# Attention: the ninth transposed block goes to spare columns of the last score bank, and VectorE's row, logit and gating work stands between its two passes

## The chip, the cores and the metric

The kernel runs on one core of one Trainium2 chip. The metric is device time in microseconds for one execution of the whole program, as the median of several runs. The engines are named as the profile names them: PE (TensorE matmul), PEld (its weight loads), DVE (VectorE), ACT (ScalarE), POOL (GpSimd), SP (the engine that issues most DMAs).

## What is computed

Three layers follow one another. The first is an attention with a threshold: 4 batches, 8 heads, 576 tokens, head size 64.

```python
scores = scale * np.matmul(q, k.transpose(0, 1, 3, 2))
thresh = np.max(scores, axis=-1, keepdims=True) - tau
scores = np.where(scores >= thresh, scores, -1000000000.0)
attn = np.exp(scores - np.max(scores, axis=-1, keepdims=True))
attn = attn / (np.sum(attn, axis=-1, keepdims=True) + 1e-09)
x = np.matmul(attn, v)            # then 2304 rows of 512
```

The second layer sends each of the 2304 rows to two of eight experts (logits of the row, noise, the best two), and the third is a dense layer with a hidden size of 2048. The change touches the attention and the choice of experts, not the matmuls of the layers behind them.

## The kernel before

The attention (the loop over `i` at L738) runs over 80 **units**. A unit is one batch, one chunk of 128 query rows and one pair of heads; 64 units have two heads (`nh` is 2), and 16 "t" units take 64 left-over rows of both heads of a pair as one tile of 128 rows (`nh` is 1). The first 16 units belong to batch 0 and have a shorter evacuation of their own (L470). Four units of one chunk make a **tile** `T` of 128 rows; there are 18 tiles.

A unit goes through these steps, each at the line named:

- `s_mm` (L350, matmuls at L364): scores of 576 columns per head, 288 in each of two PSUM banks of a `ps_s` tile. The tag has two such tiles; a two-headed unit takes both.
- `d1` (L369, DVE at L375): one pass per head reads `ps_s`, writes the scaled scores to memory and gives the row maximum. It is the only reader of `ps_s`, so it frees it for the next unit's `s_mm`.
- `a1` (L382, ACT at L386): exponentials. `thresh` (ACT, L380): the row's threshold.
- `d2` (L394, DVE at L399): the second pass, which masks by the threshold and sums the row.
- `t_mm` and `a2` (L407 and L422): the masked rows are turned by PE in blocks of 128 columns. A two-headed unit has nine blocks: parts 0 and 1 hold four each (L416), and **part 2 is the ninth block** (L418; L420 in a t unit). Each part takes a `ps_t` tile, of which the tag has three, and ACT copies it to memory (L428; L430 or L432 for the ninth block).
- `pv` (L436, PE at L449 to L454): the product with V. `group_evac` (L463) copies the finished tile out.

The steps of several units overlap, by a fixed order written out in the loop. Iteration `i` issues: `t_mm` part 0 and `a2` of unit `i - 2`, `d1` and `a1` of unit `i`, `d2` of unit `i - 1`, parts 1 and 2 of unit `i - 2`, `thresh` of `i`, `s_mm` of `i + 1`, and `pv` of `i - 3`. Every engine runs its own instructions in that order. Work beside it hangs in a table `at`, keyed by iteration and place: place 0 stands behind `s_mm`, place 1 at the end of the iteration.

For a finished tile `x_stages` (L482) puts four steps into that table, one iteration apart: `rows` (PE turns the tile at L498, DVE scales it by the inverse sums at L488, L489 and L500, SP stores it), `logits` (PE L508, ACT copy L511), `flip` (PE L515) and `sum_` (DVE L519 and L522). PE's part of each takes a `ps_t` tile too. For a group of three tiles `gating` (L532) adds the choice of experts: `top2` (DVE, L570 to L577), `rank` (PE, a `ps_t` tile) and `place` (DVE L593 and L595), then the indirect DMAs that scatter the rows (POOL L618).

After the last unit PE runs the expert and dense layers without a break to the end.

Of the kernel before, what the change touches and what calls it, by code (L numbers as in the profile page):

```python
# [14 lines left out]
HP = H // 2  # L15
# [4 lines left out]
NT = N // 128  # L20
# [5 lines left out]
DT = 2  # L26
# [7 lines left out]
def emit(tc, qt, kt, v, tau, wg, wn, noise, w1, w2, w_in, w_out, alpha, out):  # L34
# [3 lines left out]
    pe, dve, act, pool, sp = nc.tensor, nc.vector, nc.scalar, nc.gpsimd, nc.sync  # L38
# [4 lines left out]
    with (  # L43
# [56 lines left out]
        def psum_s():  # L100
            return pp.tile([128, 2, 512], FT, name="ps_s", tag="s", bufs=2)

        def psum_t(dt=FT):
            return pp.tile([128, 512], dt, name="ps_t", tag="t", bufs=3)
# [5 lines left out]
        ident = cp.tile([128, 128], FT, name="ident")  # L110
# [44 lines left out]
        rows = [c0([DM]) for _ in range(2)] + [cut(m_rows, DM * i, [DM]) for i in range(2)]  # L155
# [191 lines left out]
        NU = len(units)  # L347
        st = [dict() for _ in units]

        def s_mm(i):  # L350
            b, c, hp = units[i]
            qh, ql, kh, kl, zh, zl = sets[b * HP + hp]
            u = st[i]
            for h in range(nh(i)):
                u["ps", h] = psum_s()
            q0 = 0 if c == "t" else c * 128 + (64 if b % 2 else 0)
            for x in range(2):
                for k, (q, z, kk) in enumerate(((qh, zh, kh), (qh, zh, kl), (ql, zl, kh))):
                    for h in range(nh(i)):

                        r = slice(0, 128) if c == "t" else slice(h * 64, h * 64 + 64)
                        lhs = z if c == "t" else q[r, q0:q0 + 128]
                        o = (64 - 64 * h) + x * 288
                        pe.matmul(u["ps", h][:, x, :288], lhs, kk[r, o:o + 288], start=(k == 0), stop=(k == 2))  # L364

        def nh(i):
            return 1 if units[i][1] == "t" else 2

        def d1(i, h):  # L369
            u = st[i]  # L370
# [11 lines left out]
        def a1(i, h):  # L382
            u = st[i]
            if h == 0:
                u["em"] = em_ring()
            act.activation(u["em"][:, h], u["sp"][:, h], AF.Exp, bias=u["sm"][:, h:h + 1], scale=-1.0)  # L386
# [20 lines left out]
        def t_mm(i, part):  # L407
            u = st[i]
            em = u["em"]
            emf = em.rearrange("p h s -> p (h s)")  # L410
            ps = psum_t()
            u["pt", part] = ps
            if part < 2:
                o = part * 640
                for j in range(4):
                    pe.transpose(ps[:, j * 128:j * 128 + 128], emf[:, o + j * 128:o + j * 128 + 128], ident)  # L416
            elif nh(i) == 2:
                pe.transpose(ps[:, :128], emf[:, 512:640], ident)  # L418
            else:
                pe.transpose(ps[:64, :128], emf[:, 512:576], ident)  # L420

        def a2(i, part):  # L422
            u = st[i]
            if part == 0:
                u["P"] = pt_ring()
            ps = u.pop(("pt", part))
            if part < 2:
                act.copy(u["P"][:, 4 * part:4 * part + 4].rearrange("p a b -> p (a b)"), ps)  # L428
            elif nh(i) == 2:
                act.copy(u["P"][:, 8], ps[:, :128])  # L430
            else:
                act.copy(u["P"][:64, 8], ps[:64, :128])  # L432
# [49 lines left out]
        def x_stages(T):  # L482
            g = {}

            def inverse():
                g["inverse"] = True
                e = esum[T]
                dve.tensor_scalar(e, e, 1e-9, None, op0=OP.add)  # L488
                dve.reciprocal(e, e)  # L489

            def rows():
                x = xts[T]
                e = esum[T]
                if "inverse" not in g:
                    inverse()
                ps = psum_t()
                for c in range(HP):
                    pe.transpose(ps[:, c * 128:c * 128 + 128], x[:, c], ident)  # L498
                xtok[T] = xtok_ring()
                dve.tensor_tensor(xtok[T].rearrange("p (h d) -> p h d", h=H), ps.rearrange("p (h d) -> p h d", h=H),  # L500
                                  e[:, :, None].to_broadcast([128, H, D]), op=OP.mult)
                sp.dma_start(xd[T * 128:T * 128 + 128], xtok[T])

            def logits():
                x = xts[T]
                ps = psum_t()
                for c in range(HP):
                    pe.matmul(ps[c * 32:c * 32 + 32, :128], wcat[:, c], x[:, c], start=True, stop=True,  # L508
                              skip_group_check=True)
                g["lt"] = lt_ring()  # L510
                act.copy(g["lt"], ps[:, :128])  # L511

            def flip():
                g["ps"] = psum_t()
                pe.transpose(g["ps"][:, :128], g["lt"], ident)  # L515

            def sum_():
                t = lt_ring()
                dve.tensor_tensor(t.rearrange("p (h j) -> p h j", h=H),  # L519
                                  g["ps"][:, :128].rearrange("p (h j) -> p h j", h=H),  # L520
                                  esum[T][:, :, None].to_broadcast([128, H, 16]), op=OP.mult)
                dve.tensor_reduce(lg[:, T], t.rearrange("p (h j) -> p j h", h=H), axis=AX.X, op=OP.add)  # L522

            return [(0, 1, rows), (1, 1, logits), (2, 1, flip), (3, 0, sum_), (0, 0, inverse)]

        def bc8(ap, n):
# [5 lines left out]
        def gating(t0, t1):  # L532
# [3 lines left out]
            g = {}  # L536
# [85 lines left out]
            sends = [(T, k) for T in range(t0, t1) for k in range(2)]  # L622
            first = [exp_, one_plus, log_, noisy, top2]
            if 3 < t1 <= 12:
                plan = [(d, 1, f) for d, f in enumerate(first)] + [(5, 1, rank), (6, 0, place)]
                if t1 == FIRST:
                    plan.append((9, 0, close))
                return plan + [(6 + q, 1, lambda a=a: send(*a)) for q, a in enumerate(sends)]
            if t1 <= 15:
                plan = [(d // 2, 1, f) for d, f in enumerate(first)] + [(4, 1, rank), (5, 0, place)]  # L630
                return plan + [(5 + q // 2, 1, lambda a=a: send(*a)) for q, a in enumerate(sends)]
            if t1 == NT:

# [100 lines left out]
                f(*a)  # L734

        END = NU + DT + 1
        s_mm(0)
        for i in range(END):  # L738
            it, iv = i - DT, i - DT - 1
            tiles, outs = 0 <= it < NU, 0 <= iv < NU  # L740
            if tiles:
                t_mm(it, 0)
                a2(it, 0)
            if i < NU:
                for h in range(nh(i)):
                    d1(i, h)
                for h in range(nh(i)):
                    a1(i, h)
            if 0 < i <= NU:
                for h in range(nh(i - 1)):  # L750
                    d2(i - 1, h)
            if tiles and nh(it) == 2:
                t_mm(it, 1)
                a2(it, 1)
            if tiles:
                t_mm(it, 2)
                a2(it, 2)
            if i < NU:
                thresh(i)
            if i + 1 < NU:  # L760
                s_mm(i + 1)
            for f, a in at.pop((i, 0), []):
                f(*a)
            if i == END - 1:
                do_fill()
            if outs:
                pv(iv)
                if units[iv][2] == HP - 1 or iv < SOLO:
                    T = group_evac(iv)
                    if T is not None:  # L770
                        todo = [(i + (1, 3, 5, 7, 2)[T] + d if T < 5 else i + 1 + d, p, f) for d, p, f in x_stages(T)]
                        if T == NT - 1:
                            last_rows.append(todo[0][2])
                            todo = [(i + 1, 0, todo[1][2]), (i + 1, 0, todo[4][2]), (i + 2, 0, todo[2][2]), (i + 2, 0, todo[3][2])]
                        else:
                            todo = todo[:4]
                        if T == NT - 2:
                            todo = [(i + d, p, f[2]) for (d, p), f in zip(((1, 1), (1, 1), (2, 1), (2, 1)), todo)]
                        for t0, t1 in GROUPS:
                            if T == t1 - 1:  # L780
                                todo += [(i + {3: 8, NT - 1: 3, NT: 2}.get(t1, 4) + d, p, f) for d, p, f in gating(t0, t1)]
                        for j, p, f in todo:
                            put((j, p), f)
            if i >= NU:
                do_fill()
            for f, a in at.pop((i, 1), []):
                f(*a)
# [386 lines left out]
```

## Time and profile before

| | |
|---|---|
| median of 3 runs | 1167.44 us (1166.29 to 1167.62) |
| the profiled execution, its own time | 1170.81 us |
| its span, first to last instruction | 1169.1 us |
| PE busy | 1135.2 us (97%) |
| DVE, ACT, POOL busy | 622.8, 532.0, 532.8 us (53%, 46%, 46%) |
| granted TensorE clock, mean | 0.997 |

How it is read: the shares of busy time are averages over the attention (to about 310 us) and the layers behind it. The view by stretches gives the busy time of each engine in a stretch and the granted clock; the view of waits says who waited for whom; the timeline lists single instructions, with the idle time of the engine before them in brackets and what ended it. In a timeline a run of the same instruction is one line with its count, so the time that a step takes on PE is the distance from its start to the start of the next step.

### The profile page before, as it was taken

What the parts mean: (1) busy time and instruction counts of PE and PEld (TensorE: products, weight loads), DVE (VectorE), ACT (ScalarE), POOL (GpSimd) and SP (SyncE); (2) the same over time, 40 slices, a digit from 0 to 9 for tenths busy, and PEclk for the clock granted to TensorE, in tenths of its full rate; (3) what the DMA queues carried; (4) which work ended last, traced back from release to release, by engine and by line L of the source; (5) the groups of instructions that cost most, each with busy time, mean ns of one, the idle gap of its engine ahead of it and who ended that gap; (6) DMA issues with size and microseconds to landing.
All of it is one profiled execution on the core that took longest, in us unless ns stands there. A gap on an engine that the chain in (4) does not pass through costs nothing. (4 is left out here: it accounts for less than half of the span.)

```text
span 1169.1 us, 20453 instructions
## 1 busy us (share of the span) xinstructions
PE 1135.2 (97%) x7754; PEld 977.5 (84%) x7754; DVE 622.8 (53%) x1332; ACT 532.0 (46%) x1039; POOL 532.8 (46%) x632
## 2 busy tenths in 40 slices
PE   7999989999899999999999999999999999999997
PEld 6887777877789999999989898998888888888886
DVE  7978788899644544454545453445443343342221
ACT  7977768788624544444444454433211211211111
POOL 7636534654524545455454555556332333332221
PEclk9999999999999999999999999999999999999999
DMA  7423222132357676567667565541321321320001
GB/s 219 137 86 122 92 77 74 73 119 92 136 141 207 184 199 194 183 171 213 192 189 202 186 188 190 166 151 54 86 66 25 92 66 27 90 64 10 36 1 39
DMA packets 156552, 141.50 MB, mean 121 GB/s; under 512 B 108576, under 2 KB 109216, under 8 KB 156448
## 3 DMA queue, kind: packets, MB, share of 16 engines
q1 hardware_dynamic: 150400, 120.91, 35.1%
q0 software_dynamic: 5760, 18.88, 4.8%
q8 instruction: 63, 1.03, 0.4%
q14 instruction: 41, 0.34, 0.1%
q10 hardware_dynamic: 288, 0.34, 0.1%
HBM read 97.11 MB, written 42.99 MB: 120 GB/s over the span
## 5 line engine op out<-in xcount | busy, mean ns | idle before, releaser
L214 PE MATMUL ps_t<-m_v,m_pair 128*128 128x384 f32 (+2 forms) x1216 | 220.0, 317 | 0.3 <-DVE m_v L207 0.3
L177 POOL TENSOR_TENSOR m_pair<-m_v,m_pair 128x512 fp32r<-128x512 f32 x114 | 151.9, 1353 | 130.0 <-ACT m_pair L171 106.7
L214 PEld LDWEIGHTS ps_t<-m_v,m_pair 128*128 128x128 f32 x1216 | 186.8, 190 | 8.1 <-DVE m_v L207 0.5
L232 PE MATMUL ps_s<-m_pair,m_hh 128*128 128x512 f32 x528 | 167.5, 390 | 0.0
L995 DVE TENSOR_SCALAR m_tmp<-ps_t,alpha_t 128x512 f32<-128x512 f32 (+1 forms) x80 | 55.7, 697 | 208.6 <-PE ps_t L214 200.9
L225 DVE SCALAR_TENSOR_TENSOR m_gate<-ps_t,m_hh 128x384 fp32r<-128x384 f32 (+1 forms) x120 | 58.8, 493 | 169.9 <-ACT m_hh L224 169.8
L399 DVE SCALAR_TENSOR_TENSOR m_hh<-m_tmp,sm,m_hh 128x576 f32<-128x576 f32 x144 | 126.1, 908 | 2.4 <-ACT sm L380 2.0
L214 PE MATMUL ps_t<-m_v,m_early 128*128 128x256 f32 (+2 forms) x672 | 127.3, 320 | 0.0
L232 PEld LDWEIGHTS ps_s<-m_pair,m_hh 128*128 128x128 f32 x528 | 99.1, 188 | 20.3
L1000 POOL TENSOR_TENSOR m_v<-m_tmp,m_v 128x512 fp32r<-128x512 f32 x39 | 50.4, 1293 | 139.7 <-ACT m_v L999 139.7
L375 DVE TENSOR_SCALAR_CACHE_REDUCE m_tmp<-ps_s 128x576 f32<-128x576 f32 x144 | 103.6, 752 | 18.5 <-PE ps_s L364 16.0
L386 ACT ACTIVATE m_hh<-m_tmp,sm 128x576 f32<-128x576 f32 x144 | 105.7, 783 | 11.0 <-DVE m_tmp L375 10.9
L214 PEld LDWEIGHTS ps_t<-m_v,m_early 128*128 128x128 f32 x672 | 105.9, 189 | 5.1 <-DVE m_v L207 0.4
L364 PE MATMUL ps_s<-m_pair 64*128 64x288 f32 (+1 forms) x864 | 95.3, 318 | 12.9 <-DVE m_tmp L375 8.3
L999 ACT CAST m_v<-m_tmp 128x512 fp32r<-128x512 f32 x39 | 24.2, 620 | 173.5 <-DVE m_tmp L996 173.5
L232 PE MATMUL ps_s<-m_pair,m_gate 128*128 128x512 f32 x264 | 102.9, 390 | 0.0
L224 ACT ACTIVATE m_hh<-ps_t 128x384 fp32r<-128x384 f32 (+1 forms) x120 | 52.7, 439 | 98.3 <-PE ps_t L214 96.8
L1000 POOL TENSOR_TENSOR m_gate<-m_tmp,m_gate 128x512 fp32r<-128x512 f32 (+1 forms) x41 | 44.1, 1077 | 116.1 <-ACT m_gate L999 109.9
L364 PEld LDWEIGHTS ps_s<-m_pair 64*128 64x128 f32 (+1 forms) x864 | 72.3, 191 | 28.1 <-DVE m_tmp L375 14.3
L1019 PE MATMUL ps_s<-m_pair,m_v 128*128 128x512 f32 x396 | 95.1, 389 | 0.0
L1019 PE MATMUL ps_s<-m_pair,m_gate 128*128 128x512 f32 x360 | 88.3, 391 | 0.0
L1019 PEld LDWEIGHTS ps_s<-m_pair,m_v 128*128 128x128 f32 x396 | 74.3, 188 | 15.4
(229 smaller groups left out, 1982.0 us busy)
## 6 DMA issues: line engine op xcount, KB each, us to landing
m_v<-in_w_dram SPq DMA_DIRECT2D x64, 512.0 KB
yg<-m_tmp SPq DMA_DIRECT2D x40, 256.0 KB
m_tmp<-in_w_in_dram SPq DMA_DIRECT2D x16, 512.0 KB
m_tmp<-in_w_out_dram SPq DMA_DIRECT2D x16, 512.0 KB
m_early<-in_kt_dram SPq DMA_DIRECT2D x15, 320.0 KB
yg<-m_gate SPq DMA_DIRECT2D x18, 256.0 KB
m_rows<-xg SPq DMA_DIRECT2D x72, 64.0 KB
out_dram<-m_tmp SPq DMA_DIRECT2D x18, 256.0 KB
```

Source lines behind the costliest of these rows:

```text
L177: eng.tensor_tensor(WL[n][:, w], raw[:, w], f32(WH[n][:, w]), op=OP.subtract)
L214: pe.matmul(ps[:, :n], w[wc[d]][:, col:col + 128], x[xx][:, d, :n], start=(k == 0), stop=(k == 11))
L224: act.activation(h, ps, AF.Relu)
L225: dve.scalar_tensor_tensor(hs[1][:, f * n:f * n + n], ps, 0.0, f32(h), op0=OP.max, op1=OP.subtract)
L232: pe.matmul(ps, a[:, o:o + 128], ww[w][:, c:c + 512], start=(f == 0 and k == 0), stop=(f == nf - 1 and k == 2))
L364: pe.matmul(u["ps", h][:, x, :288], lhs, kk[r, o:o + 288], start=(k == 0), stop=(k == 2))
L375: dve.tensor_scalar(u["sp"][:, h].rearrange("p (a b) -> p a b", a=2), ps[:, :, :288], -0.125, None, op0=OP.mult, op1=OP.min, accum_out=u[" ...
L386: act.activation(u["em"][:, h], u["sp"][:, h], AF.Exp, bias=u["sm"][:, h:h + 1], scale=-1.0)
L399: dve.scalar_tensor_tensor(u["em"][:, h], u["sp"][:, h], sm[:, 2 + h:3 + h], u["em"][:, h], op0=OP.is_le, op1=OP.mult, accum_out=acc)
L995: dve.tensor_scalar(g, ps, 0.0, alpha_t[:, f:f + 1], op0=OP.min, op1=OP.mult)
L1000: pool.tensor_tensor(h[:, n:2 * n], g, f32(h[:, :n]), op=OP.subtract)
L1019: pe.matmul(ps, h[x][:, t * 128:t * 128 + 128], ww[w][:, c:c + 512], start=(f == 0 and k == 0), stop=(f == 15 and k == 2))
```

## The change

Three things move; no work is added or left out.

- Part 2 of `t_mm` takes no `ps_t` tile any more, but columns 384 to 511 of the second bank of the `ps_s` tile that the next unit's last head is about to fill (its scores take columns 0 to 287). The three last units keep the old way. For that the `ps_s` tiles of the next unit are taken before part 2, and ACT's copy of part 2 is issued behind `s_mm` and `thresh`, where it stood ahead of both.
- A new place -1 in the table stands between `d1` of unit `i` and `d2` of unit `i - 1`. For tiles 0 to 15 the DVE part of `rows` (now `scale_rows`), ACT's copy of the logits and `sum_` go there, one iteration behind the PE part; `sum_` stood behind `s_mm` in the same iteration.
- `top2` and `place` of the first five groups go to place -1 too.

```diff
@@ s_mm
-            for h in range(nh(i)):
-                u["ps", h] = psum_s()
@@ new
+        def s_bank(i):
+            for h in range(nh(i)):
+                st[i]["ps", h] = psum_s()
@@ t_mm
-            ps = psum_t()
+            ps = psum_t() if part < 2 or i + DT + 1 >= NU else st[i + DT + 1]["ps", nh(i + DT + 1) - 1][:, 1, 384:]
@@ x_stages
-            def rows():
+            def turn_rows():
                 x = xts[T]
+                g["rows"] = psum_t()
+                for c in range(HP):
+                    pe.transpose(g["rows"][:, c * 128:c * 128 + 128], x[:, c], ident)
+
+            def scale_rows():
                 e = esum[T]
                 if "inverse" not in g:
                     inverse()
-                ps = psum_t()
-                for c in range(HP):
-                    pe.transpose(ps[:, c * 128:c * 128 + 128], x[:, c], ident)
+                ps = g["rows"]
...
+            if T < NT - 2:
+                return [(0, 1, turn_rows), (1, -1, scale_rows), (1, 1, logits_mm), (2, -1, logits_copy),
+                        (2, 1, flip), (3, -1, sum_)]
             return [(0, 1, rows), (1, 1, logits), (2, 1, flip), (3, 0, sum_), (0, 0, inverse)]
@@ gating
-                plan = [(d, 1, f) for d, f in enumerate(first)] + [(5, 1, rank), (6, 0, place)]
+                plan = [(d, 1, f) for d, f in enumerate(first[:4])] + [(5, -1, top2), (5, 1, rank), (6, -1, place)]
...
-                plan = [(d // 2, 1, f) for d, f in enumerate(first)] + [(4, 1, rank), (5, 0, place)]
+                plan = [(d // 2, 1, f) for d, f in enumerate(first[:4])] + [(3, -1, top2), (4, 1, rank), (5, -1, place)]
@@ the loop over units
+        s_bank(0)
         s_mm(0)
...
                 for h in range(nh(i)):
                     a1(i, h)
+            for f, a in at.pop((i, -1), []):
+                f(*a)
...
+            if i + 1 < NU:
+                s_bank(i + 1)
             if tiles:
                 t_mm(it, 2)
-                a2(it, 2)
             if i < NU:
                 thresh(i)
             if i + 1 < NU:
                 s_mm(i + 1)
+            if tiles:
+                a2(it, 2)
```

DVE, around the scaling of a tile's rows in the middle of the attention, before (`sm_152` is the unit whose scores come next, `sm_151` the one before it, `es_144` holds the tile's row sums):

```order
L399 SCALAR_TENSOR_TENSOR m_hh,es_145<-m_tmp,sm_150,m_hh 128x576
L488 TENSOR_SCALAR es_144<-es_144 128x8
L489 RECIPROCAL es_144<-es_144 128x8 [waits DVE_49]
L500 TENSOR_TENSOR m_gate<-ps_t,es_144 128x512 [waits DMASW7_49,DMASW6_49,DMAHW3_49,DVE_49,PE_49]
L375 TENSOR_SCALAR m_tmp,sm_152<-ps_s 128x576 x2
L399 SCALAR_TENSOR_TENSOR m_hh,es_145<-m_tmp,sm_151,m_hh 128x576 [waits Activation_49]
```

The same place with the change (lines 490, 491 and 505 are the old 488, 489 and 500; 377 is 375, 401 is 399):

```order
L401 SCALAR_TENSOR_TENSOR m_hh,es_145<-m_tmp,sm_150,m_hh 128x576 x2
L377 TENSOR_SCALAR m_tmp,sm_152<-ps_s 128x576 [waits DVE_49,PE_49]
L377 TENSOR_SCALAR m_tmp,sm_152<-ps_s 128x576 [waits DVE_49,Activation_49]
L490 TENSOR_SCALAR es_144<-es_144 128x8
L491 RECIPROCAL es_144<-es_144 128x8 [waits DVE_49]
L505 TENSOR_TENSOR m_gate<-ps_t,es_144 128x512 [waits DMASW7_49,DMASW6_49,DMAHW3_49,DVE_49,PE_49]
L401 SCALAR_TENSOR_TENSOR m_hh,es_145<-m_tmp,sm_151,m_hh 128x576 x2
```

The scaling, with its waits for PE and for DMAs, stood ahead of the first pass over the next scores and now stands behind it, ahead of the second pass of the unit before. The first pass of the last head has a new wait, for ACT.

ACT, one unit in the middle of the attention, before (`sm_149` is the unit, `m_last` holds the turned blocks of the unit two before it):

```order
L428 COPY m_last<-ps_t 128x512 [waits PE_49,Activation_49]
L386 ACTIVATE m_hh<-m_tmp,sm_149 128x576 [waits DVE_49] x2
L428 COPY m_last<-ps_t 128x512 [waits PE_49,Activation_49]
L430 COPY m_last<-ps_t 128x128 [waits PE_49]
L380 ACTIVATE sm_149<-sm_149,taut 128x2
```

The same unit with the change (430, 388, 382 and 432 are the old 428, 386, 380 and 430; L527 is the copy of the logits, the old L511):

```order
L430 COPY m_last<-ps_t 128x512 [waits PE_49,Activation_49]
L388 ACTIVATE m_hh<-m_tmp,sm_149 128x576 [waits DVE_49] x2
L527 COPY m_rows<-ps_t 128x128
L430 COPY m_last<-ps_t 128x512 [waits PE_49,Activation_49]
L382 ACTIVATE sm_149<-sm_149,taut 128x2
L432 COPY m_last<-ps_s 128x128 [waits PE_49,Activation_49]
```

The copy of the ninth block has gone behind the threshold, reads `ps_s`, and its wait for PE is now for the whole group of score matmuls. The order of the matmuls on PE and of the DMAs on SP is the same as before; on POOL one pair of small copies changes place.

## Rows read from the trace of the kernel before

**Rows 1.** Stretches; us, then PE, PEld, DVE, ACT, POOL busy, granted clock, DMA.

```profile
10.00:62.00 52.00, 51.34 (x575) 43.61 (x575) 47.25 (x125) 49.11 (x114) 35.76 (x55) 1.00 0.52 154
75.00:300.00 225.00, 209.10 (x2471) 169.60 (x2467) 192.04 (x553) 174.69 (x390) 110.81 (x197) 0.99 0.28 96
330.00:1169.00 839.00, 832.27 (x4277) 728.18 (x4277) 353.05 (x556) 279.14 (x469) 355.75 (x289) 1.00 0.43 124
```

**Rows 2.** What PE waited for from 75 to 300 us: total, times, longest.

```profile
PE ps_s L364 <- DVE m_tmp L375: 6.7, 21, 0.7
PE ps_t L418 <- ACT m_tmp L428: 4.5, 11, 1.7
PE ps_t L418 <- DVE m_gate L500: 1.9, 3, 0.8
PE ps_t L418 <- ACT m_last L428: 0.7, 1, 0.7
PE ps_t L416 <- DVE m_gate L500: 0.7, 2, 0.3
PE ps_t L418 <- ACT m_rows L511: 0.6, 1, 0.6
```

**Rows 3.** Timeline of PE, a unit without waits; start, us, instruction.

```profile
208.67 1.09 PE L416 MATMUL ps_t<-ident,m_hh 128*128 128x128 f32 x8
209.59 0.27 PE L418 MATMUL ps_t<-ident,m_hh 128*128 128x128 f32 x1
...
210.78 1.09 PE L452 MATMUL ps_v<-m_tmp,m_v 128*64 128x128 f32 x16
```

**Rows 4.** Timeline of PE, a unit in which a tile's rows are scaled.

```profile
256.99 0.33 PE L418 MATMUL ps_t<-ident,m_hh 128*128 128x128 f32 x1 [0.47 <-DVE m_gate L500]
257.65 0.39 PE L364 MATMUL ps_s<-m_pair 64*128 64x288 f32 x1 [0.34 <-DVE m_tmp L375]
258.33 1.05 PE L364 MATMUL ps_s<-m_pair 64*128 64x288 f32 x11 [0.29 <-DVE m_tmp L375]
259.31 0.88 PE L452 MATMUL ps_v<-m_last,m_v 128*64 128x128 f32 x12
```

**Rows 5.** Timeline of DVE at the same unit.

```profile
255.76 0.15 DVE L488 TENSOR_SCALAR es<-es 128x8 f32<-128x8 f32 x1
...
256.85 0.75 DVE L375 TENSOR_SCALAR_CACHE_REDUCE m_tmp<-ps_s 128x576 f32<-128x576 f32 x1
...
257.52 0.75 DVE L375 TENSOR_SCALAR_CACHE_REDUCE m_tmp<-ps_s 128x576 f32<-128x576 f32 x1
```

**Rows 6.** Timeline of PE and ACT at the longest wait of part 2.

```profile
160.84 1.04 PE L416 MATMUL ps_t<-ident,m_hh 128*128 128x128 f32 x8
...
162.95 0.58 ACT L428 COPY m_tmp<-ps_t 128x512 f32<-128x512 f32 x1 [1.98 <-PE ps_t L416]
...
163.59 0.33 PE L418 MATMUL ps_t<-ident,m_hh 128*128 128x128 f32 x1 [1.71 <-ACT m_tmp L428]
```

**Rows 7.** Timeline of ACT and PE, two units of the first 62 us.

```profile
33.26 0.28 ACT L430 COPY m_last<-ps_t 128x128 f32<-128x128 f32 x1
33.42 0.32 ACT L380 ACTIVATE sm<-sm,taut 128x2 f32<-128x2 f32 x1
...
34.41 0.27 PE L418 MATMUL ps_t<-ident,m_hh 128*128 128x128 f32 x1
...
57.05 0.43 ACT L380 ACTIVATE sm<-sm,taut 128x2 f32<-128x2 f32 x1
...
57.93 0.27 PE L418 MATMUL ps_t<-ident,m_hh 128*128 128x128 f32 x1
```

**Rows 8.** Timeline of PE and ACT, a unit of the middle.

```profile
214.76 1.09 PE L452 MATMUL ps_v<-m_last,m_v 128*64 128x128 f32 x16
...
215.33 0.31 ACT L380 ACTIVATE sm<-sm,taut 128x2 f32<-128x2 f32 x1
...
216.94 0.27 PE L418 MATMUL ps_t<-ident,m_hh 128*128 128x128 f32 x1
```

More of the change, by code (lines that the diff above doesn't have):

```diff
@@ L502, in rows, with logits_mm @@
                 sp.dma_start(xd[T * 128:T * 128 + 128], xtok[T])
+            def rows():
+                turn_rows()
+                scale_rows()
             def logits():
+                logits_mm()
+                logits_copy()
+            def logits_mm():
                 x = xts[T]
                 ps = psum_t()
+                g["lp"] = ps
                 for c in range(HP):
@@ L509, in logits, with logits_copy @@
                               skip_group_check=True)
+            def logits_copy():
                 g["lt"] = lt_ring()
-                act.copy(g["lt"], ps[:, :128])
+                act.copy(g["lt"], g["lp"][:, :128])
             def flip():
@@ L774, in emit @@
                             todo = [(i + 1, 0, todo[1][2]), (i + 1, 0, todo[4][2]), (i + 2, 0, todo[2][2]), (i + 2, 0, todo[3][2])]
-                        else:
-                            todo = todo[:4]
                         if T == NT - 2:
```

## The prediction

> **What bounds the kernel now.** I read the view by stretches first. From 330 us to the end PE is busy for 832.3 of 839 us, so whatever the attention gives up or gains is carried to the end unchanged. From 75 to 300 us PE is busy for only 209.1 of 225 us, while DVE and ACT are busy for 192.0 and 174.7: nobody is full, and PE's idle time is made of short waits. From 10 to 62 us it is different: PE 51.3 of 52 us and ACT 49.1 [rows 1].
>
> The view of waits says what PE waited for in the middle stretch. There are two kinds. The score matmuls (L364) wait 6.7 us for DVE's first pass (L375), which has not yet freed the `ps_s` tiles. Parts of the transposes (L418, and L416 twice) wait 8.4 us, the sum of five rows, for a `ps_t` tile that ACT or DVE has not yet emptied [rows 2].
>
> Idle time is less than what a wait costs, because PE has to start up again. In a unit without waits PE goes from part 2 to the product with V in 210.78 - 209.59 = 1.19 us [rows 3]; where a tile's rows are scaled it takes 259.31 - 256.99 = 2.32 us, with two waits of 0.34 and 0.29 us [rows 4]. The loss is 1.13 us, 0.50 more than the idle time. The cause stands in DVE's timeline: the scaling runs from 255.76 to 256.85, and only then come the two first passes [rows 5]. For part 2 the excess is smaller: from part 0 to part 2 PE takes 0.92 us without a wait [rows 3] and 163.59 - 160.84 = 2.75 us with a wait of 1.71 [rows 6], so 0.12 us beyond the idle time.
>
> **The change part by part.**
>
> *First passes ahead of rows, logits and gating.* The 21 waits of L364 come mostly in pairs, like those of rows 4: some 10.5 pairs. They cost 6.7 + 10.5 x 0.50 = 12.0 us [rows 2, 4]. With the scaling behind the first passes, `ps_s` is free before DVE turns to it: all 12.0 us go. What is late next is the second pass of the unit before, and behind it the next unit's first pass. The scaling takes 256.85 - 255.76 = 1.09 us [rows 5]. A second pass has almost a unit of time before its transposes; the next first pass may be late by about 0.43 us, the room worked out below for the middle unit, before PE feels it. So a tile costs between 0 and 1.09 - 0.43 = 0.66 us. DVE is idle for 15% of the stretch (33 of 225 us) [rows 1], which is half a microsecond in a unit of 3.36 us (part 2 comes seven units later 23.52 us later [rows 7]), and PE has the tile's own matmuls to do meanwhile; I take 0.2 us for each of the 12 tiles that fall among two-headed units, 2.4 us, with the bounds 0 and 7.9. `top2` and `place` are moved in the same way; DVE does the same work in each unit as before, so I put them into that 0.2.
>
> *Part 2 out of the `ps_t` tiles.* The five rows are 8.4 us in 18 waits, with the start-up 8.4 + 18 x 0.12 = 10.6 us [rows 2, 6]. With two tiles per unit and three in the tag, a tile's rows or logits can hold one while parts 0 and 1 pass through the others, so these waits go. One I don't count: at 162.95 ACT began a copy after 1.98 us of idleness, although the transposes it copies had started at 160.84 and take less than a microsecond [rows 3, 6]. What it waited for is not to be seen, and may come again. That leaves 10.6 - 1.8 = 8.8 us.
>
> *The new waits.* Three instructions wait for something new. Part 2 waits for DVE's first pass over the bank it will write; behind it in PE's queue stands `s_mm`, which waited for the same pass anyway, so this costs at most the transpose's own 0.2 us where PE waits at all. ACT's copy of part 2 waits for the end of `s_mm`; behind it stand the casts and the copies of the next unit. In the middle the threshold that now precedes it starts at 215.33, and the scores ended at 214.76 [rows 8], so it finds them done. The third wait is the one that matters: the first pass over the last head waits for that copy, and the scaling and the second passes are queued behind it.
>
> Its cost is read from where ACT stands. Copy and threshold change places, so the copy ends about where the threshold ended. In the middle: 215.33 + 0.31 = 215.64. A first pass takes 0.75, and from its end to PE's start it is 258.33 - 257.52 - 0.75 = 0.06 [rows 4, 5]; with the same 0.06 from ACT to DVE, 0.87 in all, PE may go on at 216.51. Part 2 starts at 216.94 [rows 8]: 0.43 us of room, cost 0. In the first 62 us, where ACT has casts of the next batch in nearly every unit, it is late: 33.42 + 0.32 + 0.87 = 34.61 against 34.41, short by 0.20; at the end of this part 57.05 + 0.43 + 0.87 = 58.35 against 57.93, short by 0.42 [rows 7]. For the 13 two-headed units there I take the mean, 0.31: 4.0 us, with the bounds 0 (the shift may let ACT catch up) and 5.5.
>
> *Where one-headed units give way to two-headed ones*, part 2 needs a bank that a pass has only just begun to read. No row shows it; a pass step of 257.52 - 256.85 = 0.67 us [rows 5] at two of three such places is 1.3 us, with the bounds 0 and 2.0.
>
> *The rest.* The DMAs keep their order on SP; the store of a tile's rows leaves one unit later, and is read again only if an expert overflows. `place` comes a little earlier, so the scatter does too. Matmuls, copies and passes are the same in number and size.
>
> Sum: 12.0 + 8.8 - 2.4 - 4.0 - 1.3 = **13.1 us less**. The profiled execution took 1170.8 us, 3.4 more than the median 1167.4; from it the sum gives 1157.7, and for the median **1154.3 us**.
>
> **A rule that speaks against it.** The trace of before has the copy of the ninth block beside the next scores, in another bank, at no cost to PE [rows 3, 7]. The Trainium skill, "PSUM — Partial Sum Buffer", section "PSUM bank collisions raise a hardware error", says that no two engines may use one bank in the same partitions at once, two readers included, and that software must keep them apart. The wait of the first pass for ACT is that rule at work, and by it the copy and the pass stand in series in every unit, which is the third rival below (1168.6 us); by the rows of the middle the copy is over in time. No run here shows it yet.
>
> **The rivals.**
>
> 1. *More of it*: the early units cost nothing, because ACT slides into place, and DVE's lag is absorbed. Then 13.1 + 4.0 + 2.4 = 19.5 us go: 1147.9. For it: ACT's idle tenths in the middle. Chance 0.20.
> 2. *The `ps_t` waits form again*, since rows and logits now hold their tile for a unit longer while `rank` takes one too. Then 8.8 us less are gained, 4.3 in all: 1163.1. For it: five groups with `rank`; against it: two tiles per unit instead of three. Chance 0.17.
> 3. *Copy and pass in series everywhere*: 0.28 us for the copy [rows 7] in the other 51 two-headed units is 14.3 us, which eats the gain: 1168.6, no change. Against it: the room of 0.43. Chance 0.06.
> 4. *Slower*: the new wait ties DVE to ACT, and ACT, delayed by DVE in turn, stays as late in all units as at 57 us: 0.42 us in 51 more units is 21.4 us, 8.3 net: 1175.7. It decides from 13.1 / 51 = 0.26 us per unit, that is when ACT stands 0.7 us later than in rows 8. For it: rows 7; against it: ACT has 50 us of idle time in the middle [rows 1], in the first part 3. Chance 0.07.
>
> That the attention gains and the end does not move I don't hold likely: PE is full behind it [rows 1].
>
> **How the numbers follow.** The forecast has 0.50. Differences within 0.2%, 2.3 us, are about what a measurement of this kernel can tell from none. Faster are the forecast and rivals 1 and 2: 0.87; same is rival 3: 0.06; slower is rival 4: 0.07. With all bounds at their best the gain is 12.0 + 10.6 = 22.6 us, and the granted clock of 0.99 in the middle [rows 1] could give back up to 1% of 225 us, 2.2 more; at their worst it is 20.8 - 7.9 - 5.5 - 2.0 = 5.4 us. The range takes in rivals 1 and 2 and leaves out the others and the far ends: 1146 to 1163.5.
>
> **What would show it.** If the steps are right, PE's waits for L375 and for `ps_t` from 75 us on fall from 15 us to a few, no unit shows two waits inside its score matmuls behind a scaling, and from 19 to 59 us units take 3.5 to 3.8 us instead of 3.36. New waits should be DVE for ACT's copy of the ninth block, about 0.2 us each, and PE's part 2 for L375. The forecast is wrong if part 0 or 1 still waits for a scaling, if DVE's waits for that copy are over half a microsecond in the middle, or if the stretch behind the attention grows.

## The result and the profile after

| | before | with the change |
|---|---|---|
| median (lowest to highest), us | 1167.44 (1166.29 to 1168.07) | 1154.86 (1154.50 to 1155.12) |
| profiled execution, us | 1170.81 | 1154.86 |
| its span, us | 1169.1 | 1153.1 |
| mean granted clock of its span | 0.997 | 0.999 |

The ratio is 0.9894, with a 95% interval of 0.9883 to 0.9905: 12.6 us less. The forecast was 1154.3, in the range 1146 to 1163.5. The two profiled executions differ by 16.0 us, because the one of before took 3.4 us longer than its median.

Lines move by the change: 364, 375, 399, 416, 418, 428, 430, 380, 500, 511, 593 are now 362, 377, 401, 418, 420, 430, 432, 382, 505, 527, 612; the product with V is L454 and L456 (L452 and L454 before). So L418 is part 2 in the rows of before, and parts 0 and 1 with the change.

Stretches of the kernel with the change; us, then PE, PEld, DVE, ACT and POOL busy, granted clock, DMA. The attention ends some 16 us earlier, so the middle is read to 290 us.

```profile
10.00:62.00 52.00, 51.00 (x570) 43.17 (x570) 46.91 (x121) 48.55 (x112) 37.43 (x54) 1.00 0.53 154
75.00:290.00 215.00, 204.43 (x2524) 168.85 (x2525) 196.93 (x563) 176.24 (x399) 110.48 (x202) 1.00 0.29 101
330.00:1153.00 823.00, 816.36 (x4191) 714.56 (x4189) 348.34 (x536) 275.45 (x461) 353.66 (x286) 1.00 0.43 124
```

Beside [rows 1], PE's idle time in the middle has fallen from 15.9 to 10.6 us, and the granted clock is 1.00 instead of 0.99. These stretches don't hold the same work. From the 20th unit's product with V to the last one's they do; before, then with the change:

```profile
79.94:319.83 239.89, 220.63 (x2579) 179.32 (x2578) 197.95 (x571) 183.10 (x408) 121.24 (x210) 0.99 0.28 96
80.50:303.64 223.14, 211.48 (x2578) 174.82 (x2577) 200.42 (x574) 180.17 (x407) 119.25 (x212) 1.00 0.29 104
```

Of the 16.75 us between them, 7.6 are idle time of PE (19.3 against 11.7) and 9.15 are time in which PE is recorded as busy, with the same matmuls. What PE still waits for from 75 to 290 us (total, times, longest):

```profile
PE ps_s L362 <- DVE m_tmp L377: 5.1, 17, 0.4
PE ps_t L418 <- DVE m_gate L612: 1.9, 3, 0.7
PE ps_t L418 <- ACT m_last L430: 1.4, 1, 1.4
PE ps_s L420 <- DVE m_tmp L377: 0.7, 1, 0.7
PE ps_t L418 <- DVE m_hh L401: 0.6, 2, 0.4
```

Against [rows 2]: no wait for a scaling (L505) and none for the logits' copy is left. But the waits for the first pass are 17, not none; they are single ones of 0.4 us at most, where before most came in pairs. And the positions of `rank` (L612) still hold up part 1. The wait of 1.4 us for ACT isn't new: it stands at 289.09 us, and before has it too, behind the 300 us at which [rows 2] end:

```profile
304.61 0.66 PE L416 MATMUL ps_t<-ident,m_hh 128*128 128x128 f32 x4 [1.42 <-ACT m_last L428]
```

What DVE waits for in the same stretch:

```profile
DVE m_tmp L377 <- ACT m_last L432: 6.1, 11, 1.3
DVE m_tmp L377 <- ACT m_last L434: 3.9, 3, 1.4
DVE m_tmp L377 <- ACT m_tmp L434: 1.5, 5, 0.5
```

These are the new waits for the copy of the ninth block. A unit in which a tile is scaled, to be laid beside [rows 4, 5]; DVE first, then PE:

```profile
115.18 0.76 DVE L377 TENSOR_SCALAR_CACHE_REDUCE m_tmp<-ps_s 128x576 f32<-128x576 f32 x1 [0.23 <-ACT m_last L432]
...
116.96 0.69 DVE L505 TENSOR_TENSOR m_gate<-ps_t,es 128x512 f32<-128x512 f32 x1
```

```profile
116.38 0.27 PE L420 MATMUL ps_s<-ident,m_hh 128*128 128x128 f32 x1
116.58 1.06 PE L362 MATMUL ps_s<-m_pair 64*128 64x288 f32 x12
117.57 1.09 PE L454 MATMUL ps_v<-m_last,m_v 128*64 128x128 f32 x16
```

The first pass ends at 115.94, the scaling runs after it, and PE goes from part 2 to the product with V in 1.19 us without a wait. Before, a scaling made that 2.32 us.

The early units, where the forecast saw a price; ACT, DVE and PE of the unit that answers to the first half of [rows 7]:

```profile
33.90 0.31 ACT L382 ACTIVATE sm<-sm,taut 128x2 f32<-128x2 f32 x1
34.09 0.27 ACT L432 COPY m_last<-ps_s 128x128 f32<-128x128 f32 x1
```

```profile
34.39 0.76 DVE L377 TENSOR_SCALAR_CACHE_REDUCE m_tmp<-ps_s 128x576 f32<-128x576 f32 x1
```

```profile
35.04 0.27 PE L420 MATMUL ps_s<-ident,m_hh 128*128 128x128 f32 x1
35.25 1.05 PE L362 MATMUL ps_s<-m_pair 64*128 64x288 f32 x12
```

Copy, pass and part 2 stand end to end, and PE loses nothing: part 2 begins at 35.04 although the pass is recorded until 35.15.

Unit by unit, the start of the product with V comes later than before by 0.3 us over the first 14 units, which the 15th gives back (and by 0.55 us once, at the very first, which another kernel with the same early code doesn't show). From there to the one-headed units (80 to 222 us) the change gains 14.4 us, in those units nothing, after them 2.3 us more. Behind the attention nothing moves.

One spot of before isn't in the prediction's sum. Its DVE and PE, then PE's clock there with what PE did ahead of its fall:

```profile
118.48 0.69 DVE L500 TENSOR_TENSOR m_gate<-ps_t,es 128x512 f32<-128x512 f32 x1 [3.08 <-DMA xg<-m_gate,posi]
...
119.23 0.33 PE L418 MATMUL ps_t<-ident,m_hh 128*128 128x128 f32 x1 [0.63 <-DVE m_gate L500]
119.91 0.40 PE L364 MATMUL ps_s<-m_pair 64*128 64x288 f32 x1 [0.35 <-DVE m_tmp L375]
120.58 1.24 PE L364 MATMUL ps_s<-m_pair 64*128 64x288 f32 x11 [0.28 <-DVE m_tmp L375]
```

```profile
119.00:120.00 1.00, 0.42 (x2) 0.23 (x2) 1.00 (x4) 0.12 (x1) 0.57 (x3) 1.00 0.03 8
120.00:121.00 1.00, 0.72 (x7) 0.51 (x9) 1.00 (x3) 1.00 (x2) 0.73 (x3) 1.00 0.91 285
121.00:122.00 1.00, 1.00 (x11) 0.72 (x11) 1.00 (x5) 1.00 (x4) 1.00 (x1) 0.65 0.86 236
122.00:123.00 1.00, 1.00 (x12) 1.00 (x12) 1.00 (x4) 0.17 (x1) 0.78 (x3) 0.50 1.01 401
123.00:124.00 1.00, 1.00 (x12) 0.75 (x8) 1.00 (x3) 0.00 (x0) 0.46 (x1) 0.50 0.56 225
124.00:125.00 1.00, 1.00 (x13) 0.54 (x12) 0.84 (x4) 0.19 (x1) 0.00 (x0) 0.65 0.64 262
```

A scaling stood for 3.08 us, at the end for a scatter of gating (the transposes that it reads were done by 117.7 us), and both first passes stood behind it. PE waited 1.26 us in all, was busy for 0.42, then 0.72 of a microsecond, and then its granted clock fell to 0.50 (1.2 instead of 2.4 GHz) for about three microseconds. That is 1.7 us (0.35 + 0.50 + 0.50 + 0.35) beyond the waits. With the change the granted clock doesn't fall anywhere in the attention.

### The profile page after: what moved, and what is told of

Same layout as the page of the kernel before. It is cut to its first block, busy times and chain, and to the rows that moved or that the text cites. A ratio compares the mean times of both kernels' runs of the same rounds, so it can differ in the third digit from the quotient of the medians.

```text
span 1153.1 us, 20565 instructions
## 1 busy us (share of the span) xinstructions
PE 1126.6 (98%) x7754; PEld 973.3 (84%) x7754; DVE 624.7 (54%) x1332; ACT 529.1 (46%) x1039; POOL 532.9 (46%) x632
## 5 line engine op out<-in xcount | busy, mean ns | idle before, releaser
L401 DVE SCALAR_TENSOR_TENSOR m_hh<-m_tmp,sm,m_hh 128x576 f32<-128x576 f32 x144 | 125.4, 903 | 0.0
L362 PE MATMUL ps_s<-m_pair 64*128 64x288 f32 (+1 forms) x864 | 88.9, 318 | 12.2 <-DVE m_tmp L377 7.1
L362 PEld LDWEIGHTS ps_s<-m_pair 64*128 64x128 f32 (+1 forms) x864 | 69.3, 192 | 26.0 <-DVE m_tmp L377 16.5
```

Of the source, the lines that this page charges most:

```text
L401: dve.scalar_tensor_tensor(u["em"][:, h], u["sp"][:, h], sm[:, 2 + h:3 + h], u["em"][:, h], op0=OP.is_le, op1=OP.mult, accum_out=acc)
```

## The experiments

All were timed against the kernel before. They ran in three sets of four, each set on one chip, and the medians of before were 1167.47, 1169.96 and 1172.15 us; so sets are compared by ratios, kernels of a set by times.

### First set: the two halves of the change

**The bank alone.** Part 2 goes to `ps_s`, its copy stands behind the scores; rows, logits and gating keep the order of before.

```diff
-                return [(0, 1, turn_rows), (1, -1, scale_rows), (1, 1, logits_mm), (2, -1, logits_copy),
-                        (2, 1, flip), (3, -1, sum_)]
+                return [(0, 1, rows), (1, 1, logits), (2, 1, flip), (3, 0, sum_)]
...
-                plan = [(d, 1, f) for d, f in enumerate(first[:4])] + [(5, -1, top2), (5, 1, rank), (6, -1, place)]
+                plan = [(d, 1, f) for d, f in enumerate(first)] + [(5, 1, rank), (6, 0, place)]
...
```

> Only the ninth block's move to the score bank; scaling, logits copy, sum_, top2 and place stay where they were before the change. Theory A (two independent parts, as in the sum of the prediction): the 8.8 us of waits for ps_t tiles go, the 12.0 us of waits of L364 for the first pass stay, early units cost next to nothing: about 1159 us. Rival (the two parts need each other: a wait taken from part 2 comes back at the score matmuls, because the scaling still stands ahead of the first pass): at most 2 us gained, 1165 or more, and PE's waits of the score matmuls for the first pass grow above 8 us.

Measured: 1173.63 us, ratio 1.0049 (1.0036 to 1.0063): slower by 6.2 us, the rival, and beyond it. PE's waits from 75 to 290 us:

```profile
PE ps_s L420 <- DVE m_tmp L377: 12.7, 13, 1.9
PE ps_s L362 <- DVE m_tmp L377: 8.1, 22, 0.9
PE ps_t L418 <- DVE m_gate L505: 0.7, 2, 0.3
```

The `ps_t` waits are nearly gone, as foreseen, but part 2 now waits for the first pass over the last head where DVE work stands ahead of the passes. At six scalings, where before mostly had two waits of 0.35 and 0.28 us inside the scores, it waits 0.67 us, and the scores 0.29. Where `top2` stands ahead, as at 149.80 us, part 2 waits 1.46 us and the scores 0.35; before lost 0.40 us in that unit (148.99 to 150.58 instead of 1.19).

**The order alone.** DVE's work stands between the passes; part 2 stays in a `ps_t` tile and is copied at once.

```diff
-            ps = psum_t() if part < 2 or i + DT + 1 >= NU else st[i + DT + 1]["ps", nh(i + DT + 1) - 1][:, 1, 384:]
+            ps = psum_t()
...
             if tiles:
                 t_mm(it, 2)
+                a2(it, 2)
...
-            if tiles:
-                a2(it, 2)
```

> Only the DVE order (place -1); part 2 takes a ps_t tile and is copied at once, as before the change. Theory A (independent parts): 12.0 less 2.4 us are gained, about 1158 us. Rival (the parts need each other: a tile's rows now hold one of three ps_t tiles for a unit longer while three parts per unit go round, so part 2 waits for the scaling, half a microsecond or more per tile): 1163 us or more, and PE waits at part 2 or part 0 for the line of the scaling some 12 times.

Measured: 1161.22 us, ratio 0.9944 (0.9931 to 0.9958): a gain of 6.2 us, between the two expectations. PE's waits from 75 to 290 us, the larger ones:

```profile
PE ps_t L420 <- DVE m_gate L505: 4.9, 7, 1.3
PE ps_t L420 <- ACT m_last L430: 2.8, 10, 0.3
PE ps_t L420 <- DVE m_rows L535: 1.3, 2, 0.8
PE ps_t L418 <- DVE m_gate L612: 1.2, 2, 0.6
```

No score matmul waits for a pass any more; part 2 waits for `ps_t` tiles instead, which rows and logits now hold for longer. So neither half has a fixed worth: the bank costs 6.2 us in the old order and gains 6.4 in the new one (5.8 by the ratios), and the order gains 6.2 us without the bank and 18.8 with it.

**The copy of the ninth block done twice**, in all 80 units. Nothing is left out.

```diff
                 act.copy(u["P"][:, 8], ps[:, :128])
+                act.copy(u["P"][:, 8], ps[:, :128])
             else:
+                act.copy(u["P"][:64, 8], ps[:64, :128])
                 act.copy(u["P"][:64, 8], ps[:64, :128])
```

> The changed kernel with ACT's copy of the ninth block done twice, so that each first pass over a last head is released about 0.2 us later. If there is room in the middle units (0.43 us by the prediction), the 0.2 us are felt only where DVE already waits for that copy: 0 to 3 us more, 1155 to 1158 us. If copy and pass stand in series in every unit (the prediction's third and fourth rivals), 64 units pay 0.2 us: about 1168 us.

Measured: 1161.01 us, ratio 0.9941 (0.9928 to 0.9953): 6.15 us more than the change. Unit by unit, eight of the first 14 pay some 0.3 us each, 2.4 in all, and behind them about one in three pays 0.1 to 0.3, 4.0 in all. Between the two expectations: the copy isn't in series with the pass everywhere, but the room of 0.43 us in the middle isn't there in every unit. A rival stays: the second copy also fills ACT, which is busy for 191.4 of the 220 us from 75 us on, against 176.2 of 215 with the change, and no run gave ACT the same work at another place.

**The rank earlier.** In three of the groups its matmuls go to the place behind part 2's copy, and the positions are taken at the end of the same iteration.

```diff
-                plan = [(d, 1, f) for d, f in enumerate(first[:4])] + [(5, -1, top2), (5, 1, rank), (6, -1, place)]
+                plan = [(d, 1, f) for d, f in enumerate(first[:4])] + [(5, -1, top2), (5, 0, rank), (5, 1, place)]
```

> The changed kernel with rank behind s_mm (ahead of the product with V) and place at the end of the same iteration, for the three middle groups, so that rank's ps_t tile is free before the next unit's part 1. If part 1's three waits of 0.6 to 0.7 us for place are a real cost of the ring, they go: about 1152.5 us. Rival (place ahead of the next first passes delays them by as much): 1154.5 to 1156 us.

Measured: 1154.33 us, ratio 0.9883 (0.9866 to 0.9899). PE's wait for L612 falls from 1.9 to 0.7 us, and the time is 0.5 us lower, near the rival's range and not clear of the change's interval here; the third set settles it.

### Second set: pieces of the order

**The scaling alone behind the passes.** The sum over heads, `top2` and `place` stand ahead of the first passes again; the bank is moved.

```diff
-                        (2, 1, flip), (3, -1, sum_)]
+                        (2, 1, flip), (3, 0, sum_)]
...
-                plan = [(d, 1, f) for d, f in enumerate(first[:4])] + [(5, -1, top2), (5, 1, rank), (6, -1, place)]
+                plan = [(d, 1, f) for d, f in enumerate(first)] + [(5, 1, rank), (6, 0, place)]
...
```

> The change with only the scaling of the rows behind the first passes; the sum over heads, top2 and place stand ahead of the first passes, as before. Theory A (the scaling, with its wait for transposes that are issued behind part 2, is what made the old order expensive together with the bank move): 1155 to 1158. Rival B (every piece of DVE work ahead of the first passes costs its length, some 0.3 to 0.6 us in 12 tiles and 5 groups): 1159 to 1163.

Measured: 1167.76 us, ratio 0.9983 (0.9974 to 0.9992). Worse than either expectation: without these small pieces, which the prediction had put into 0.2 us a tile, most of the gain is gone. (So it is without the scaling, as the third set shows.) One place, DVE, then PE, then PE's clock:

```profile
142.81 0.29 DVE L589 MAX8 mx<-m_gate 128x8 f32<-128x8 f32 x3
...
143.89 0.75 DVE L377 TENSOR_SCALAR_CACHE_REDUCE m_tmp<-ps_s 128x576 f32<-128x576 f32 x1
```

```profile
144.70 0.33 PE L420 MATMUL ps_s<-ident,m_hh 128*128 128x128 f32 x1 [1.51 <-DVE m_tmp L377]
145.38 1.81 PE L362 MATMUL ps_s<-m_pair 64*128 64x288 f32 x12 [0.35 <-DVE m_tmp L377]
```

```profile
143.00:144.00 1.00, 0.19 (x2) 0.00 (x0) 0.93 (x11) 0.29 (x1) 0.00 (x0) 1.00 0.00 0
144.00:145.00 1.00, 0.30 (x1) 0.14 (x1) 1.00 (x3) 0.32 (x1) 0.00 (x0) 1.00 0.00 0
145.00:146.00 1.00, 0.65 (x5) 0.62 (x6) 1.00 (x5) 1.00 (x2) 0.00 (x0) 0.64 0.00 0
146.00:147.00 1.00, 1.00 (x10) 0.84 (x8) 0.80 (x4) 0.80 (x3) 0.00 (x0) 0.50 0.00 0
```

`top2` takes 1.1 us ahead of the passes (142.81 to 143.89), behind the sum over heads, which began at 142.20; part 2 waits 1.51 us for the pass over the last head, and then the clock falls to half, so that the same 12 score matmuls take 1.81 us instead of 1.06.

**The copy of the ninth block ahead of the threshold.**

```diff
-            if i < NU:
-                thresh(i)
             if i + 1 < NU:
                 s_mm(i + 1)
             if tiles:
                 a2(it, 2)
+            if i < NU:
+                thresh(i)
```

> The change, but ACT copies the ninth block before it takes the threshold of the next unit instead of after it, so the copy ends some 0.2 us earlier in every unit. Doubling the copy cost 6.15 us over all units (1161.0 against 1154.9). Theory A, the coupling is a two-sided slope (each tenth that the copy ends later or earlier moves the first pass of the last head, and about a quarter of that reaches PE): 1151 to 1153.5. Rival B, the coupling only costs beyond a room that the change does not use up: no gain, 1154.3 to 1155.5. Rival C, the threshold, now later, holds up the second pass: over 1156.

Measured: 1156.97 us, ratio 0.9887 (0.9872 to 0.9902). By the ratio 0.8 us better than the change, inside the interval. The early units give 0.3 us, and behind them the traces show little: nearer to rival B.

**Both of these.** The rank earlier and the copy ahead of the threshold.

> Both the copy ahead of the threshold and the rank one place earlier (which alone gave 1154.3): the candidate for the best version. If the two are independent it is 0.5 us below the kernel with the copy ahead of the threshold; if that one gains nothing, 1154 to 1154.8.

Measured: 1155.73 us, ratio 0.9880 (0.9865 to 0.9895), 1.2 us below the one with the copy alone, more than the 0.5 expected.

**The copy of the logits where it was.**

```diff
-                return [(0, 1, turn_rows), (1, -1, scale_rows), (1, 1, logits_mm), (2, -1, logits_copy),
+                return [(0, 1, turn_rows), (1, -1, scale_rows), (1, 1, logits_mm), (1, 1, logits_copy),
```

> The change, but the copy of the logits stands where it stood before, behind the ninth block's copy of the unit in which the logits are computed, and not behind the scalings of the next unit. Theory A (the middle has room on ACT, and what the logits' copy delays is the copy of the next unit's ninth block in one place as in the other): 1154.5 to 1156. Rival B (the logits' copy waits for PE there, and the unit's own scalings and copies stand behind it): 1157 to 1160, with PE waits for a ps_t tile of 3 us or more.

Measured: 1157.35 us, ratio 0.9891 (0.9875 to 0.9906), no difference to the change; 0.4 us of waits for that copy (L527) in all. Splitting the logits' copy from its matmuls has no share in the gain. (The times expected were those of the first chip; by the ratio it is theory A.)

### Third set: the change again, and two that beat it

**The change itself.**

> The change itself, once more, as the neighbour of the other three on the same chip. Its ratio to the kernel before was 0.9894 (0.9883 to 0.9905); 0.9885 to 0.9900 is expected again.

Measured: 1158.66 us (1158.10 to 1159.34), ratio 0.9887 (0.9872 to 0.9902).

**The rank earlier, beside it.**

> The rank one place earlier, beside the change on the same chip. Theory (the wait of parts of the transposes for the positions, 1.9 us, is what it removes, and half a microsecond of it comes back elsewhere): 0.3 to 1.0 us below the change. Rival (the earlier difference was that of two sets of runs): within 0.2 us of it or above.

Measured: 1157.26 us (1156.95 to 1158.00), ratio 0.9875 (0.9860 to 0.9891): 1.4 us below the change, more than expected.

**The rank earlier and the copy ahead of the threshold.**

> The rank earlier and the copy of the ninth block ahead of the threshold. Theory (the copy gives some tenths in the first fifty units of time and nothing after, as its trace showed): 0.5 to 1.5 us below the change, and up to 0.6 below the kernel with the rank alone. Rival (the copy earlier is worth nothing): equal to the kernel with the rank alone.

Measured: 1156.01 us (1155.23 to 1156.99), ratio 0.9862 (0.9847 to 0.9877): 2.65 us below the change, with no overlap between the two sets of times, and 1.25 below the rank alone, more than either expectation. It is the best version of these runs. By the medians the earlier copy is worth about a microsecond after all, though the slowest time of the two together (1156.99) just passes the fastest of the rank alone (1156.95).

**All but the scaling.** The complement of the run with the scaling alone.

```diff
-                return [(0, 1, turn_rows), (1, -1, scale_rows), (1, 1, logits_mm), (2, -1, logits_copy),
+                return [(0, 1, rows), (1, 1, logits_mm), (2, -1, logits_copy),
```

> The complement of the run with the scaling only: the sum over heads, top2 and place are moved as in the change, the scaling of the rows stays ahead of the first passes, with the transposes that it reads issued right before it. Theory A (both halves are needed, each piece that stays ahead of the passes now delays part 2, which the bank move hangs on the last pass): 1160 to 1166, and PE's waits of part 2 for the first pass stand at the scalings, 8 us or more of them. Rival B (the scaling was not the costly part, since PE can hide 1.1 us): 1155 to 1158.

Measured: 1172.55 us, ratio 1.0005 (0.9996 to 1.0014). Theory A, and beyond its range. PE's waits from 75 to 290 us, and the worst place, DVE and PE:

```profile
PE ps_s L420 <- DVE m_tmp L377: 10.0, 9, 2.2
PE ps_s L362 <- DVE m_tmp L377: 7.9, 20, 1.2
```

```profile
118.75 0.69 DVE L505 TENSOR_TENSOR m_gate<-ps_t,es 128x512 f32<-128x512 f32 x1 [2.21 <-DMA xg<-m_gate,posi]
...
120.26 0.45 PE L420 MATMUL ps_s<-ident,m_hh 128*128 128x128 f32 x1 [2.23 <-DVE m_tmp L377]
```

The scaling stands again at the head of DVE's queue and waits for the scatter; part 2 waits 2.23 us, and from 120 to 127 us the granted clock is 0.50 to 0.56.

With the bank moved, in ratios: nothing of DVE's work behind the first passes 1.0049, all but the scaling 1.0005, the scaling alone 0.9983, everything 0.9894. The steps are 0.0044 and 0.0066 each by itself, 0.0155 together: some 40% more than their sum.

## Why the prediction was right, and where only in its total

**First passes ahead (12.0 us less 2.4).** The mechanism is shown: the double waits behind a scaling are gone, and pieces left ahead of the passes cost. The size is not: 17 single waits remain. One of 0.35 us costs 0.41 to 0.48 (part 2 to the product with V takes 1.60 to 1.67 us instead of 1.19), so with 5.1 us of idle time some 6.8 are left of the 12.0. The step that failed is "all 12.0 us go", with 0.2 us a tile for DVE's lag: over the 12 tiles the lag is nearer to 0.6, inside its bounds. What is late next was named rightly, the second pass and behind it the next first pass. In eight of the 17 places a second pass of 1.4 us or more stands ahead (below), in three `top2`, in four a scaling. One of the eight, DVE and PE with the change:

```profile
183.06 0.76 DVE L377 TENSOR_SCALAR_CACHE_REDUCE m_tmp<-ps_s 128x576 f32<-128x576 f32 x1 [0.62 <-ACT m_last L432]
...
185.15 1.41 DVE L401 SCALAR_TENSOR_TENSOR m_hh<-m_tmp,sm,m_hh 128x576 f32<-128x576 f32 x1
...
187.98 1.07 PE L362 MATMUL ps_s<-m_pair 64*128 64x288 f32 x12 [0.35 <-DVE m_tmp L377]
```

And putting `top2` and `place` into that 0.2 was wrong: the two runs with part of the order show that the small pieces decide nearly as much as the scaling (0.0089 and 0.0111 of the ratio, each taken away last).

**Part 2 out of the `ps_t` tiles (8.8 us).** The waits for scaling and logits went. The waits for `rank` stayed, as a small part of rival 2 (1.9 us). Without the 1.4 us for ACT, which [rows 2] don't count in before, 3.2 us of `ps_t` and part 2 waits, 3.9 with the start-up, are left of 10.6. The wait of 1.71 us in [rows 6], of which the prediction said that it may come again, is not in this trace (one like it came in the third set, below). That these 8.8 us and the 12.0 were added as two terms is the deeper error: the bank alone is 6.2 us slower. The sum held because the change has both, and that is luck: nothing in the prediction says that the halves need each other.

**The early units (4.0 us).** Measured 0.3 in all. The chain from ACT's copy by the pass to PE is there, end to end, but my link from the pass's end to PE's start, 0.06 us, was too long by about 0.2: PE began part 2 0.11 us before the pass is recorded to end (35.04 against 35.15). Doubling the copy makes eight of these units pay 0.3 us each, so the margin is small. Copying ahead of the threshold takes the 0.3 us away. Two of the places that the price was read from don't show it: the part 2 at 57.93 and at 216.94 [rows 7, 8] stand ahead of a one-headed unit, whose scores of 128 rows follow them. There part 2 needs the bank of the first head's pass, which waits for no copy. At the second ACT is idle for a microsecond, so the room of 0.43 us was read from an easy place.

**The transitions (1.3 us).** No part 2 waits for a pass there; the score matmuls wait 0.26 and 0.38 us in a unit soon after (88.21 and 229.47). The one wait of part 2 for a pass, 0.7 us at 243.62, stands behind a second pass of 1.83 us and 1.3 us of `close`, a step of the choice of experts.

**The new wait in the middle (0).** DVE's waits for the copy are longer than the 0.2 us foreseen, 11.5 us in the three rows, and up to 1.4. Over half a microsecond was the prediction's own sign that it is wrong. Two of its signs of being right failed too: PE's waits fell from 15 us to 9.7 and not to a few, and the early units took no 3.5 to 3.8 us. The total held all the same. Not every wait for the copy reaches PE: behind the 1.28 us at 212.61 PE doesn't wait. But seven of the waits (0.2 to 0.6 us, 1.1 at the last) stand ahead of PE's wait in the next unit, as at 183.06 above, five of them together with a long second pass, and no run separates the two. What one copy costs is therefore open; about a microsecond of it goes when the copy stands ahead of the threshold. Rival 3's mechanism is at work: at 34 us the copy ends at 34.36 and the pass begins at 34.39. The trace agrees there with the rule that the prediction took from the Trainium skill ("PSUM — Partial Sum Buffer", section "PSUM bank collisions raise a hardware error"). As its price, rival 3 had 0.28 us in 51 units, 14.3 us; the units behind the early ones pay 4.0 for a second copy.

**Not in the sum.** The wait for the scatter at 118 us and the clock behind it: 1.7 us of clock alone. The view of DVE's waits would have shown it. It fits that before's times scatter with the clock: beside the first set they go from 1166.2 us at a mean granted clock of 0.998 to 1170.7 at 0.994, while the change's five stay within 0.6 us at 0.998 to 1.000. The spot doesn't explain the 3.4 us between the profiled execution of before and its median: beside the first set, executions at the profiled one's clock, 0.997, took 1166.9 to 1168.4 us. A rival is the chip, since the median of before is 1167.5, 1170.0 and 1172.2 us on the three of the sets; on which chip it was profiled isn't recorded. So the 3.4 us stay open, and the 16.0 may hold them.

Together: 12.0 - 6.8 = 5.2, 10.6 - 3.9 = 6.7, clock 1.7, and the first unit's later start -0.55 (the 0.3 of the early units come back), in all 13.1 of the 16.0 us between the two profiled executions. Of the other 2.9, some 1.8 lie in units where part 2 to the product with V takes longer than 1.19 us without a wait that the profile lists (3.0 us in before, 1.2 with the change); the rest stays unassigned. The forecast's 13.1 came within 0.5 of the 12.6 between the medians by luck: the gain was over-counted (9.6 and 8.8 us were forecast, 5.2 and 6.7 are found), the price too (5.3 us, of which 0.8 at most is found), and the clock wasn't counted. These errors offset each other.

## What to carry to other kernels

Work moved behind a pass and a bank shared with that pass can't be priced one by one: a tile that hangs on the last pass can turn an instruction ahead of that pass into a wait for PE, down to a `top2` of 1.1 us, and the same tile is worth 6.4 us once that work stands elsewhere. Look in the waits of the in-order engine that frees the tiles, not only in those of the bottleneck: behind the 3.08 us that end with a scatter PE waited 1.26 us and then lost 1.7 by the clock. And where a chain has little slack left, tenths count: test it by doubling a link before calling its room free. When two profiles are compared, lay them over the same work, not over the same microseconds: a wait at 304.61 us in one and at 289.09 in the other looked new.

## What was unexpected of the hardware

**Second passes beside POOL.** From 60 to 300 us 13 of 115 second passes (L401) take 1.34 to 1.92 us instead of 0.81, and 14 of 109 in before. All 27 lie beside a TENSOR_TENSOR of POOL for at least 0.7 us, though 14 and 12 of the usual length do too. One of them, DVE and POOL with the change:

```profile
201.11 1.42 DVE L401 SCALAR_TENSOR_TENSOR m_hh<-m_tmp,sm,m_hh 128x576 f32<-128x576 f32 x1
```

```profile
199.69 2.21 POOL L316 TENSOR_TENSOR m_pair<-m_early,m_pair 128x320 fp32r<-128x320 f32 x2 [2.92 <-ACT m_pair L308]
```

No run took POOL's work away, so this is a coincidence in time, not a shown cause.

**ACT idle without a visible reason.** At 163 us of before [rows 6] and at one place of the change in the third set, ACT stays idle though the four transposes that it copies are done. The second, PE and ACT:

```profile
149.63 1.09 PE L418 MATMUL ps_t<-ident,m_hh 128*128 128x128 f32 x8
```

```profile
152.84 0.58 ACT L430 COPY m_last<-ps_t 128x512 f32<-128x512 f32 x1 [4.25 <-PE ps_s L362]
```

The copy reads the first four of these eight transposes, which are done 0.65 us after the start, at 150.28, yet it begins at 152.84; in [rows 6] it begins 1.5 us after them. The same program's first trace has an idle time at the same place, but there the copy follows the fourth transpose by 0.1 us (150.70 and 150.79), so a long idle time alone shows nothing.

A packet of the instruction queue q14 moves half a microsecond before the 4.25 us begin (between 148.0 and 148.5 us). One moves at the same place in the first trace (148.5 to 149), where the copy isn't late, so it explains nothing by itself. What ACT waits for stays open.
